# One row of a Fourier stage as three products side by side in column quarters, added up by a 96-row table in the next stage

## Chip, core, metric

The kernel runs on one core of one Trainium2 chip. The metric is the device time of one execution in microseconds (us), median of several. TensorE is called PE below, as in the profile; DVE is VectorE, ACT ScalarE, POOL GpSimd.

## The reference, cut to what matters

Block-sparse attention for 4 batches, 8 heads, 768 positions, head size 64; its output, 768 x 512 for each batch, then goes through a Fourier mix and a small network. Only the Fourier mix is touched:

```python
X = np.fft.fft(x, axis=1)            # along the sequence, 768
X = np.fft.fft(X, axis=2)            # across the model dimension, 512
mixed = np.real(X).astype(np.float32)
u = x + mixed
```

## The kernel before

For each batch, `along` multiplies folded inputs with cosine and sine tables of the sequence, and `across` multiplies the result with tables of the model dimension. Folding halves the columns twice; one column is left over, number QD = DM/4 = 128. Its row is called `side`, takes four products that accumulate, and enters `across` as a one-row product with the table `alt`. The parts concerned (cuts are marked):

```python
alt = const.tile([1, QD + 1], FP32, name="alt")
# ... setting up the tables, on VectorE:
for to, frm in ((dst, raw), (alt, row)):
    nc.vector.tensor_copy(out=to[:, 0:1], in_=frm[:, KD - 1:KD])
    nc.vector.tensor_copy(out=to[:, 1:QD + 1], in_=frm[:, 0:KD - 2:2])
# ...
parts = (slice(DM - QD, DM), slice(0, QD), slice(QD, QD + 1))
def along(g):                                   # g = 0, 1 cosine; 2, 3 sine
    # ...
    def cosine(ps, rows, cols):
        mm = nc.tensor.matmul
        for t in (0, 2):
            mm(ps[rows, 0:KS], sa[:, t, cols], cs_sb[:, t, :], start=(t == 0), stop=False)
        mm(ps[rows, 0:odd], e1[:, cols], cs_sb[:, 1, 0:odd], start=False, stop=False)
        mm(ps[rows, odd:KS], sa[:, 1, cols], cs_sb[:, 1, odd:KS], start=False, stop=True)
    # ...
    if g == 2:
        side = ps_m.tile([P, 512], FP32, tag="m", name="side")
        at = bank("m")
        cosine(side, slice(0, 1), parts[2])     # one column of weights
        st["zs"] = room(0, [P, 2, KS], "zs")
    # ... sine products into ps, copy of ps into zs
    if g == 2:
        keep_cosine(zs[0:1, 0, :], side[0:1, :])
        give(at, busy("PE", 2.0) + 1.5)

def across_p(ps, rows, ks):
    zc, zl = st["zc"], st["zs"][0:1, 0, :]
    mm = nc.tensor.matmul
    mm(ps[rows, 0:QD + 1], zc[:, 0, ks], cd_sb[:, 0:QD + 1], start=True, stop=False)
    mm(ps[rows, 0:QD + 1], zl[:, ks], alt, start=False, stop=True)
    mm(ps[rows, QD + 1:KD], zc[:, 1, ks], cd_sb[:, QD + 1:KD], start=True, stop=True)

def across(m):                                  # three planes of 128 positions
    # ...
    across_p(ps, slice(0, P), ks)
    if m == 1:
        end = ps_t.tile([P, 512], FP32, tag="t", name="end")
        across_p(end, slice(0, 1), slice(KS - 1, KS))   # the last row, by itself
```

## Time and profile before

| | before |
|---|---|
| median of the 3 runs at hand when predicting | 1147.89 us (1145.8 to 1148.28) |
| span of the profiled run | 1143.0 us |
| PE busy | 1091.1 us, 95% |
| VectorE, ScalarE, GpSimd busy | 56%, 34%, 22% |
| PE in the chain that ended last | 87% |

The page gives busy shares and the chain; the time view gives single stretches. The lines on which this rests are in the prediction, which also explains their columns.

### The profile page before, as it was taken

How to read it: one execution, taken by the hardware profiler on the slowest of the kernel's cores; microseconds unless marked ns; L12 is line 12 of the kernel's file. 1: busy time of each engine (PE TensorE's matmuls, PEld its weight loads, DVE VectorE, ACT ScalarE, POOL GpSimd, SP SyncE). 2: the span in 40 equal slices, each digit the busy share in tenths (PEclk: the TensorE clock that was granted, in tenths of full speed). 3: DMA queues.
4: the chain of work that ended last, by engine and by line, in shares of the span. 5: the costliest groups of instructions: out<-in, count | busy, mean ns of one | idle time of the engine just before them, and what ended most of it. 6: DMA issues, size and time to landing. Idle time of an engine off the chain costs nothing.

```text
span 1143.0 us, 11972 instructions
## 1 busy us (share of the span) xinstructions
PE 1091.1 (95%) x4284; PEld 518.3 (45%) x4284; DVE 643.2 (56%) x1190; ACT 391.6 (34%) x809; POOL 250.2 (22%) x182
## 2 busy tenths in 40 slices
PE   6999988979899999999999999999999999999997
PEld 2333333433445555454454555444444555544553
DVE  3888879488764544554459455544456355533431
ACT  3887755545212012344443112244330202201110
POOL 1000067457300000243536100243440001000000
PEclk9999999989899999999999999999999999999999
DMA  6657322011000000211111000111000001000002
GB/s 194 185 162 228 96 55 56 15 41 44 1 0 1 1 0 6 61 31 42 33 24 28 0 1 1 48 50 29 1 1 0 1 1 28 28 1 0 1 0 58
DMA packets 65184, 44.27 MB, mean 39 GB/s; under 512 B 52814, under 2 KB 57948, under 8 KB 65116
## 3 DMA queue, kind: packets, MB, share of 16 engines
q1 hardware_dynamic: 63228, 42.62, 13.1%
q10 hardware_dynamic: 1856, 0.79, 0.3%
q8 instruction: 36, 0.59, 0.2%
q14 instruction: 32, 0.26, 0.1%
q0 software_dynamic: 32, 0.01, 0.0%
HBM read 37.11 MB, written 6.29 MB: 38 GB/s over the span
## 4 chain that ended last, share of the span: by engine, by line
PE 87%; DVE 7%; ACT 3%; issue 2%; POOL 1%; DVEq 0%; ACTq 0%; POOLq 0%
PE y L932 29%; PE z L879 14%; PE s L468 11%; PE o L510 9%; PE yp L879 7%; PE xp L879 4%; DVE e L489 3%; PE tp L438 2%; PE zp L691 1%; PE sp L557 1%; PE xt L528 1%; PE s L473 1%; PE zp L669 1%; DVE x L744 1%; PE utp L806 1%
## 5 line engine op out<-in xcount | busy, mean ns | idle before, releaser
L498 POOL TENSOR_TENSOR acc<-acc,e 128x768 f32<-128x768 f32 x96 | 179.4, 1868 | 111.6 <-DVE e L489 107.0
L468 PE MATMUL s<-qT,kT 64*128 64x384 f32 x768 | 165.1, 535 | 13.9 <-DVE e L489 10.6
L935 DVE TENSOR_TENSOR x<-y,x 128x512 f32<-128x512 f32 x96 | 66.3, 691 | 196.6 <-PE y L932 196.4
L489 DVE TENSOR_TENSOR e<-s,mask 128x768 f32<-128x768 f32 x144 | 131.2, 951 | 73.9 <-ACT s L487 73.9
L932 PE MATMUL y<-w_sb,hB 128*128 128x512 f32 x384 | 170.2, 594 | 1.1 <-DVE x L935 1.0
L932 PE MATMUL y<-w_sb,hA 128*128 128x512 f32 x384 | 170.6, 593 | 0.6 <-ACT zs L693 0.6
L510 PE MATMUL o<-e,vr 128*64 128x384 f32 x768 | 146.1, 502 | 0.0
L487 ACT ACTIVATE s<-s 128x768 f32<-128x768 f32 x144 | 109.4, 794 | 68.4 <-PE s L468 67.3
L932 PEld LDWEIGHTS y<-w_sb,hB 128*128 128x128 f32 x384 | 71.5, 190 | 86.8 <-issue 81.9
L932 PEld LDWEIGHTS y<-w_sb,hA 128*128 128x128 f32 x384 | 71.2, 190 | 82.5 <-issue 79.5
L884 DVE TENSOR_TENSOR hA<-z,hA 128x384 f32<-128x384 f32 x64 | 35.7, 558 | 121.9 <-PE z L879 121.9
L496 POOL TENSOR_TENSOR acc<-e 128x768 f32<-128x768 f32 x24 | 46.3, 1928 | 248.8 <-DVE e L489 188.6
L468 PEld LDWEIGHTS s<-qT,kT 64*128 64x128 f32 x768 | 63.9, 190 | 74.9 <-DVE e L489 28.1
L879 PE MATMUL z<-unT,t 128*128 128x384 f32 x256 | 93.0, 486 | 0.0
L757 POOL TENSOR_SCALAR st<-st 128x1 f32<-128x1 f32 x24 | 6.6, 274 | 355.2 <-DVE st L756 354.8
L510 PEld LDWEIGHTS o<-e,vr 128*64 128x64 f32 x768 | 47.0, 137 | 76.8 <-issue 75.1
L888 ACT ACTIVATE hA<-hA 128x384 f32<-128x384 f32 x64 | 33.4, 522 | 119.4 <-DVE hA L884 118.8
L879 PEld LDWEIGHTS z<-unT,t 128*128 128x128 f32 x256 | 48.6, 190 | 33.9
L888 ACT ACTIVATE hB<-hB 128x384 f32<-128x384 f32 x64 | 33.5, 523 | 85.2 <-DVE hB L884 85.2
L899 ACT COPY hA<-xp 128x384 f32<-128x384 f32 x32 | 15.3, 478 | 134.4 <-PE xp L879 134.4
L879 PE MATMUL xp<-unT,w_sb 128*128 128x384 f32 x128 | 48.5, 502 | 1.5 <-ACT zs L693 1.1
L879 PE MATMUL yp<-unT,w_sb 128*128 128x384 f32 x128 | 47.1, 491 | 0.2 <-DVE un L726 0.2
(173 smaller groups left out, 1243.1 us busy)
## 6 DMA issues: line engine op xcount, KB each, us to landing
wraw<-in_moe_w_ch_dram SPq DMA_DIRECT2D x32, 512.0 KB
qr<-in_q_dram SPq DMA_DIRECT2D x90, 64.0 KB
vr<-in_v_dram SPq DMA_DIRECT2D x30, 192.0 KB
kr<-in_k_dram SPq DMA_DIRECT2D x28, 192.0 KB
out_dram<-x SPq DMA_DIRECT2D x16, 128.0 KB
out_dram<-x SPq DMA_DIRECT2D x8, 256.0 KB
out_dram<-x SPq DMA_DIRECT2D x8, 126.0 KB
out_dram<-x SPq DMA_DIRECT2D x4, 252.0 KB
```

Of the source, the lines that this page charges most:

```text
L438: nc.tensor.transpose(tp[:, c * P:(c + 1) * P], part, ident)
L468: nc.tensor.matmul(s[:, i, 0:HS], kT[D * i:D * i + D, c * P:(c + 1) * P], qT[D * i:D * i + D, half * HS:(half + 1) * HS], start=True, stop ...
L487: nc.scalar.activation(out=s[:, :, 0:HS], in_=s[:, :, 0:HS], func=ACT.Exp, scale=scale)
L489: nc.vector.tensor_tensor(out=e, in0=s[:, :, 0:HS], in1=m.broadcast_to([P, 2, HS]), op=ALU.mult)
L496: nc.gpsimd.tensor_add(out=acc_of[n, half], in0=e_of[u - 1], in1=e)
L498: nc.gpsimd.tensor_add(out=acc_of[n, half], in0=acc_of[n, half], in1=e)
L510: nc.tensor.matmul(o[D * i:D * i + D, :], vt[:, i, c, :], e[:, i, :], start=(c == 0), stop=(c == C - 1))
L879: nc.tensor.matmul(to, a[:, k, :], c[:, k, :], start=(k == 0), stop=(k == ND // 2 - 1))
L884: tt(out=to, in0=ps, in1=a, op=ALU.add)
L888: nc.scalar.activation(out=h, in_=h, func=ACT.Relu)
L932: nc.tensor.matmul(y, hs[half][:, l, m * P:(m + 1) * P], w2_sb[:, 4 * r + l, :], start=(l == 0), stop=(l == 3))
L935: nc.vector.tensor_tensor(out=x[:, m, :], in0=y, in1=x[:, m, :], op=ALU.add)
```

## The change

The four products of `side` no longer accumulate in one output. The first two and the pair of half-length ones go to three quarters of the array's columns (output partitions 0, 32 and 64), where they can run at once; 32 weight columns each are loaded, of which one matters. The three partial rows are added by the next stage's product: `alt` gets 96 rows, with the table in rows 0, 32 and 64 and zeros elsewhere. The intent is to shorten the 2 us of `side`.

```diff
-    alt = const.tile([1, QD + 1], FP32, name="alt")
+    alt = const.tile([96, QD + 1], FP32, name="alt")
...
-                for to, frm in ((dst, raw), (alt, row)):
+                nc.vector.memset(alt, 0.0)
+                for to, frm in ((dst, raw), *((alt[g:g + 1, :], row) for g in (0, 32, 64))):
...
-                cosine(side, slice(0, 1), parts[2])
-                st["zs"] = room(0, [P, 2, KS], "zs")
+                for i, (lhs, t, cols) in enumerate(((sa[:, 0, :], 0, slice(0, KS)),
+                                                    (sa[:, 2, :], 2, slice(0, KS)),
+                                                    (e1, 1, slice(0, odd)),
+                                                    (sa[:, 1, :], 1, slice(odd, KS)))):
+                    g32 = 32 * min(i, 2)
+                    nc.tensor.matmul(side[g32:g32 + 32, cols], lhs[:, QD:QD + 32],
+                                     cs_sb[:, t, cols], start=True, stop=True,
+                                     tile_position=(0, g32))
+                st["zs"] = room(0, [P, 3, KS], "zs")
...
-                keep_cosine(zs[0:1, 0, :], side[0:1, :])
-                give(at, busy("PE", 2.0) + 1.5)
+                keep_cosine(zs[0:96, 2, :], side[0:96, :])
+                give(at, busy("PE", 0.8) + 1.5)
...
-            zc, zl = st["zc"], st["zs"][0:1, 0, :]
+            zc, zl = st["zc"], st["zs"][0:96, 2, :]
```

More of the change, by code (lines that the diff above doesn't have):

```diff
@@ L653, in fourier @@
                  lambda: fold_1(1), lambda: fold_2(0), lambda: fold_2(2), lambda: fold_2(1)]
-        parts = (slice(DM - QD, DM), slice(0, QD), slice(QD, QD + 1))
+        parts = slice(DM - QD, DM), slice(0, QD)
         def along(g):
```

## The prediction

> **What bounds the kernel now.** I read the page first: the busy shares and the chain that ended last.
>
> ```profile
> PE 1091.1 (95%) x4284; PEld 518.3 (45%) x4284; DVE 643.2 (56%) x1190; ACT 391.6 (34%) x809; POOL 250.2 (22%) x182
> ...
> PE 87%; DVE 7%; ACT 3%; issue 2%; POOL 1%; DVEq 0%; ACTq 0%; POOLq 0%
> ```
>
> TensorE (PE) is busy in 95% of 1143.0 us and carries 87% of the chain. A microsecond taken from it should mostly come off the end, except where it waits for someone else. I took the busy time by stretches to see where that is.
>
> ```profile
> 180.00:370.00 190.00, 170.11 (x729) 83.26 (x728) 132.08 (x199) 73.92 (x159) 74.70 (x49) 0.96 0.09 21
> 370.00:560.00 190.00, 189.39 (x692) 92.07 (x690) 93.71 (x181) 54.27 (x110) 43.58 (x34) 1.00 0.10 25
> 560.00:860.00 300.00, 296.61 (x1156) 143.70 (x1154) 162.98 (x275) 100.19 (x207) 97.66 (x61) 1.00 0.07 18
> 860.00:940.00 80.00, 79.02 (x240) 40.72 (x241) 40.32 (x91) 11.02 (x27) 1.56 (x4) 1.00 0.00 1
> ```
>
> After the length of a stretch comes busy PE. From 370 us on, PE is 99% busy; only 180 to 370 us has 20 us of PE idleness. The changed code runs once per batch: batch 0 at 203 to 261 us, inside that loose stretch; batches 1, 2 and 3 at 338 to 387, 638 to 687 and 888 to 937 us, in full ones (at 338 to 387 us PE waits once, 0.57 us).
>
> Next, PE in order of time around one `side` (the single row DM/4), batch 3. Columns: start, length to the end of the last matmul, line, rows*columns of the weights, shape, count. An fp32 matmul shows as two passes. I use differences of starts, because ends overlap.
>
> ```profile
> 902.21 1.45 PE L879 MATMUL z<-unT,t 128*128 128x384 f32 x4
> 903.59 1.45 PE L669 MATMUL side<-cs_sb,sa 128*1 128x385 f32 x4
> 904.89 0.49 PE L670 MATMUL side<-cs_sb,e 128*1 128x192 f32 x2
> 905.21 0.49 PE L671 MATMUL side<-cs_sb,sa 128*1 128x193 f32 x2
> 905.63 2.20 PE L691 MATMUL zp<-sn_sb,sd 128*128 128x384 f32 x6
> ```
>
> One useful weight column holds PE from 903.59 to 905.63: 2.04 us. Then PE around the next stage, one plane with the extra row `end`:
>
> ```profile
> 934.05 0.39 PE L701 MATMUL pq<-cd_sb,zc 128*128 128x129 f32 x2
> 934.36 0.48 PE L702 MATMUL pq<-alt,zs 1*128 1x129 f32 x2
> 934.78 0.49 PE L703 MATMUL pq<-cd_sb,zc 128*128 128x128 f32 x2
> 935.20 0.38 PE L701 MATMUL end<-cd_sb,zc 128*1 128x129 f32 x2
> 935.51 0.38 PE L702 MATMUL end<-alt,zs 1*1 1x129 f32 x2
> 935.81 0.38 PE L703 MATMUL end<-cd_sb,zc 128*1 128x128 f32 x2
> 936.12 0.49 PE L716 MATMUL pq<-sd_sb,zs 128*128 128x127 f32 x2
> 936.45 0.39 PE L718 MATMUL pq<-sd_sb,zs 128*128 128x128 f32 x2
> 936.67 1.13 PE L879 MATMUL xp<-unT,w_sb 128*128 128x384 f32 x3
> ```
>
> Two passes of 128 columns from L718 to the next line take 0.22 us (936.45 to 936.67). The same work around the one-row `alt` product takes 0.31, 0.42 and 0.42 us: PE loses time wherever the weights' shape changes, about 0.1 us before and 0.1 us after.
>
> **What the Trainium skill says.** "TensorEngine Tiling (Array Packing)", Key Properties, says that different tiles load and multiply in parallel and that changing the tiling mode, not just the tile, drains TensorE. The trace agrees: 0.22 against 0.42 us above. The built program gives `alt` a 32x128 tile before and 128x128 after, its neighbours 128x128 in both; for `end`, 32x32 becomes 128x32, again as its neighbours have. "TensorE: Matmul & The Clock Gate", Part 3, Measured speedup, gives 2.38x for three column tiles of 32. This trace has four such tiles:
>
> ```profile
> 48.79 0.85 PE L557 MATMUL sp<-e,pick 128*32 128x384 f32 x8
> 49.58 0.33 PE L314 MATMUL m<-at_q,at_k 24*128 24x384 bf16 x1
> ```
>
> Eight passes of 384 columns in 0.79 us; one after another they would take 8 x 0.3225 = 2.58 us (0.3225 is the spacing in the `side` row: (904.89 - 903.59) / 4), so 3.3x with four different moving operands. The same page, LDWEIGHTS, has load time go by the columns of the weights, not by the rows contracted. The trace agrees: 181 ns for the 1x128 loads of `alt`, 190 for 128x128 ones. So 96 rows in place of one should cost some 9 ns a load.
>
> **The change part by part.**
> 1. `side`. Removed, per batch: 2.04 us. Added: three products in column quarters 0, 1 and 2, two of 385 columns, and 192 then 193 columns in the third. Each quarter streams two passes of 385 columns' worth, 2 x 0.3225 = 0.645 us. Adding the exposed weight load and drain that `sp` shows (0.79 - 0.645 = 0.14) gives 0.79 us if all three run beside each other. If the third quarter's passes had to keep order with the others, I estimate its four would end about 0.16 us later, 0.95 us. I take 0.81: saved 1.23 us, four times, **4.9 us**.
> 2. `alt` in the planes. L701, L702, L703 now have one mode. A plane that follows 128x128 work and precedes L716 takes 0.31 + 0.42 + 0.32 = 1.05 us before (the last without the drain towards `end`); with six passes at 0.108 it takes 0.65. Saved 0.40 us; the drain towards `end` and entries from 128x64 work stay and cancel. Three planes, four batches: 12 x 0.40 = **4.8 us**. The diff does not mention this; it comes from the tile size alone.
> 3. `alt` in `end`: 0.31 + 0.31 + 0.31 becomes 0.22 + 0.22 + 0.31, 0.18 us x 4 = **0.7 us**.
> 4. ScalarE copies `side` out with 96 rows for one: 480 ns where it was 470, 263 where 252 (`zc`'s 128-row copies against `zs`'s one-row copies). About 20 ns a batch, beside PE.
> 5. VectorE at about 132.8 us: a memset of 96x129 and four more small copies. Each existing pair starts 0.2 us after the one before; with 0.2 assumed for the memset, 0.6 us once, in a stage where VectorE runs ahead of what PE needs. I charge 0.3.
>
> The order of instructions on all engines in the part that runs is otherwise unchanged: the scheduler's smaller figure for `side` (0.8 for 2.0) reorders nothing there. Sum on PE: 4.9 + 4.8 + 0.7 = 10.4 us.
>
> **What of it reaches the end.** Batches 1 to 3 stand in full PE work: all 3 x 2.6 = 7.8 us. In batch 0 the chain in order of time goes through PE from 200 to 223 us, through `side` and the first plane, then by ScalarE to VectorE's mask product; both start earlier, so 1.6 us should pass. The second plane at 237.5 us leads into GpSimd's sums and statistics, the third at 258 us is on PE's chain: I count half of the second and all of the third, 0.2 + 0.6. Sum: 7.8 + 2.4 - 0.3 = 9.9 us; I take off another 0.4 for waits that reappear: **9.5 us**, 1147.89 - 9.5 = 1138.4 us, 0.8%.
>
> **The rivals.**
> - *The packing doesn't pack.* Had the two products in the third quarter, or three weight loads of 32 columns, to run one after another, `side` would stay near 2.0 us and only the 5.5 us of mode changes would come: about 1143 us. Against it: `sp` packs already.
> - *Only packing counts, mode changes are no loss.* If the 0.1 us before and after `alt` came from the accumulation or the read of the one-row tile and not from its shape, the planes would keep 1.05 us: 4.9 us saved, about 1143.5 us. Against it: `end`, surrounded by other shapes, shows the same 0.1 us at each of its edges.
> - *A wait takes its place.* After `side`, PE waits for the copy of `zs` (0.57 us in batches 1 and 3), and before 300 us scores wait for VectorE's mask product:
>
> ```profile
> PE s L468 <- DVE e L489: 10.6, 9, 1.9
> ```
>
> If VectorE, 98% busy from 224 to 236 us, sets the pace of batch 0, most of its 2.6 us is lost: 1140.5 us. For it: the chain is on VectorE for part of this stage. The 0.57 us wait is a fixed distance behind the sine product and moves with it.
> - *The clock.* PE idleness near 245 us coincides with a granted clock of 0.81 from 248 to 262 us. Shifting it may move the time 1 to 2 us either way.
>
> **Range and chances.** The gain runs from about 5 (one of the first two rivals) to about 11 us (all passes, no loss), and the runs of the kernel before spread by 2.5 us. I say 1138.4 us, 8 in 10 between 1134.0 and 1143.5. Two per cent is 23 us, more than twice all the PE time at stake, so faster by over 2% gets 0.01; slower by over 2% would need a new stall of 23 us with the order unchanged, 0.01.
>
> **What would show it.** In the changed profile: from the start of `side` to the start of the sine product 0.75 to 0.95 us where it was 2.04; in the planes 0.22 us (0.31 after 128x64 work) from the `zc` product to `alt`, 0.22 from `alt` to the next, and no 0.42; in `end` the first two steps 0.22; PE busy some 9 to 11 us lower; the wait after the sine product still about 0.57 us; 20 us of PE idleness in the 180 to 370 us stretch grown by no more than about 1 us. The prediction is wrong if `side` keeps 2 us, if planes keep 1.05 us, or if idle time before scores grows by what PE saved.

## The result, and the profile after

The changed kernel took 1133.82 us (median of 4 runs, 1131.42 to 1136.86) against 1146.85 us (4 runs, 1143.91 to 1148.28): ratio 0.9891, 95% interval 0.9859 to 0.9923. A ratio here is the mean time of one kernel's fast runs over the mean of the other's in the same rounds, so not quite the ratio of the medians.

First the page of the changed kernel: PE's share stays at 95%, with 11.7 us less busy time.

```profile
PE 1079.4 (95%) x4284; PEld 516.3 (46%) x4284; DVE 643.9 (57%) x1195; ACT 391.4 (35%) x809; POOL 250.1 (22%) x182
```

Then PE in order of time around `side` of batch 3:

```profile
895.23 0.52 PE L695 MATMUL side<-cs_sb,sa 128*32 128x385 f32 x2
895.24 0.51 PE L695 MATMUL side<-cs_sb,e 128*32 128x192 f32 x2
895.57 0.51 PE L695 MATMUL side<-cs_sb,sa 128*32 128x385 f32 x4
896.01 2.20 PE L701 MATMUL zp<-sn_sb,sd 128*128 128x384 f32 x6
898.78 0.70 PE L942 MATMUL y<-w_sb,hA 128*128 128x512 f32 x1 [0.57 <-ACT zs L703]
```

Two first passes of 385 columns and the third quarter's first start within some 20 ns (895.23, 895.24); the long quarters' second passes follow at 895.57, and the sine product starts at 896.01: 0.78 us after `side` began, where it was 2.04. The wait after the sine product is still 0.57 us. And the planes of batch 3, with the first rows of `end`:

```profile
923.65 0.39 PE L711 MATMUL pq<-cd_sb,zc 128*128 128x129 f32 x2
923.88 0.39 PE L712 MATMUL pq<-alt,zs 96*128 96x129 f32 x2
924.10 0.39 PE L713 MATMUL pq<-cd_sb,zc 128*128 128x128 f32 x2
924.41 0.38 PE L711 MATMUL end<-cd_sb,zc 128*1 128x129 f32 x2
924.63 0.39 PE L712 MATMUL end<-alt,zs 96*1 96x129 f32 x2
```

The steps are 0.23 and 0.22 us where they were 0.31 and 0.42. The `alt` weights are now 96*128 for 1*128 and cost no more. The 0.31 us before `end`, whose single column is still another shape, is left.

To see where the 10.8 us between the two traces come from, I cut each at fixed instructions (starts read from the views by time). A slot is one step of the attention loop. The same was done for a second trace of each, taken later:

| stretch | before | after | difference | second pair |
|---|---|---|---|---|
| start to the third slot's first scores | 25.00 | 22.10 | -2.90 | -2.06 |
| to `side` of batch 0 | 185.95 | 186.73 | +0.78 | +1.67 |
| to `side` of batch 1 | 140.66 | 139.47 | -1.19 | -2.86 |
| to `side` of batch 2 | 299.75 | 297.28 | -2.47 | -2.47 |
| to `side` of batch 3 | 252.24 | 249.65 | -2.59 | -2.58 |
| to the end of batch 3's planes | 33.08 | 30.49 | -2.59 | -2.59 |
| to the end | 206.29 | 206.43 | +0.14 | +0.18 |
| sum | 1142.96 | 1132.15 | -10.82 | -10.71 |

Two things stand out. Batches 1 to 3 give nearly the same amount each. And the first 25 us, in which nothing was changed, give more than any batch. That, and the loss just after it, had to be explained.

### The profile page after: what moved, and what is told of

Its sections match the earlier page's. It is cut to its first block, busy times and chain, and to the rows that moved or that the text cites. A ratio compares the mean times of both kernels' runs of the same rounds, so it can differ in the third digit from the quotient of the medians.

```text
span 1132.1 us, 11978 instructions
## 1 busy us (share of the span) xinstructions
PE 1079.4 (95%) x4284; PEld 516.3 (46%) x4284; DVE 643.9 (57%) x1195; ACT 391.4 (35%) x809; POOL 250.1 (22%) x182
## 4 chain that ended last, share of the span: by engine, by line
PE 85%; DVE 8%; ACT 2%; issue 2%; DMA 1%; SPq 1%; POOL 1%; ACTq 0%; DVEq 0%; POOLq 0%
PE y L942 29%; PE z L889 15%; PE s L470 10%; PE o L512 8%; PE yp L889 7%; PE xp L889 4%; DVE e L491 3%; PE tp L440 2%; PE zp L701 1%; PE sp L559 1%; DMA wraw<-in_moe_w_ch_dram 1%; PE xt L530 1%; PE zp L672 1%; PE s L475 1%; PE sp L573 1%
```

## The experiments

**My theory.** The change takes about 2.6 us of PE time a batch in two parts that have nothing to do with each other: packing (1.25 us) and the end of shape changes around `alt` (1.33 us). The rest of the first rounds' 13 us is chance in the start-up. **Rivals.** Packing alone is the gain; shape changes alone are it; the start-up belongs to the change. All runs have 5 rounds beside the kernel before.

| run | median us (range), 6 runs | ratio to before (95%) |
|---|---|---|
| after_again | 1134.76 (1133.7 to 1137.28) | 0.9926 (0.9904 to 0.9948) |
| before_again | 1141.61 (1141.17 to 1144.52) | 0.9984 (0.9962 to 1.0005) |
| pack_only, wrong result | 1140.79 (1137.06 to 1146.37) | 0.9973 (0.9945 to 1.0001) |
| mode_only | 1138.14 (1135.8 to 1141.58) | 0.9957 (0.9932 to 0.9981) |
| flat | 1137.93 (1135.22 to 1138.33) | 0.9937 (0.9914 to 0.9960) |
| end_wide | 1136.24 (1132.76 to 1138.17) | 0.9927 (0.9903 to 0.9952) |
| warm | 1131.25 (1130.05 to 1135.76) | 0.9899 (0.9873 to 0.9924) |
| best | 1131.83 (1129.34 to 1136.97) | 0.9901 (0.9874 to 0.9928) |
| pool_alt | 1134.61 (1131.75 to 1137.16) | 0.9902 (0.9871 to 0.9932) |
| best_all | 1129.74 (1128.8 to 1131.72) | 0.9863 (0.9834 to 0.9893) |
| warm_before | 1139.94 (1139.05 to 1143.64) | 0.9964 (0.9933 to 0.9996) |

The first four rows share a chip and its runs of before (11, median 1144.02), the next four another (1144.52), the last three a third (1144.55).

### after_again and before_again: the two kernels once more

No edit. 

> The changed kernel once more, unaltered. Theory: the change takes 10.5 us of TensorE time (4 x 1.25 in the side row, 12 x 0.40 in the planes, 4 x 0.18 in the end row), of which 9.5 to 10.5 us reach the end, so a ratio of 0.990 to 0.992; the 12.5 us of the first rounds holds 2 to 3 us of run-to-run start-up difference, already there in the two traces before the first changed instruction (side of batch 0 starts at 208.8 us against 210.95). Rival: the change is worth 12.5 us or more by itself, ratio 0.989 again.

> The kernel before against itself, for the size of the noise and for a second trace of it. Theory: ratio 1.000 within 0.003; the start of batch 0's side row in this trace differs from 210.95 us by up to 2 or 3 us although nothing was changed, and the distances within batches 1 to 3 are the same to 0.05 us. Rival: batch 0's side row starts at 210.9 again, and then the changed kernel's earlier start has to be explained by the change.

The changed kernel came out at 0.9926, 8.5 us, a little short of the expected 0.990 to 0.992, which the interval of 5.9 to 11 us still holds; before against itself at 0.9984. Over all rounds and chips, the 10 runs of the changed kernel have a mean of 1134.70 us and the 43 of before 1144.21: 9.5 us. The runs of before go from 1141.2 to 1149.0. That the start of before's trace would differ was a miss: batch 0's `side` began at 210.84 us, after 210.95 in the first trace. On that reading my start-up theory could have fallen. But the changed kernel's two traces differ among themselves (208.83 and 210.45 us), and the next runs' traces have 212.07 and 207.67, above and below both. `warm` and `warm_before` below settled it.

### pack_only: packing without the shape

```diff
-            zc, zl = st["zc"], st["zs"][0:96, 2, :]
+            zc, zl = st["zc"], st["zs"][0:1, 2, :]
-            mm(ps[rows, 0:QD + 1], zl[:, ks], alt, start=False, stop=True)
+            mm(ps[rows, 0:QD + 1], zl[:, ks], alt[0:1, :], start=False, stop=True)
```

> The changed kernel with the next stage's product on one row of the packed result only (so a wrong result on purpose): the three products side by side stay, the 32x128 tile of the row product returns. Theory of two separate parts: side row 0.78 us, row product with 0.42 us steps again; 4.5 to 5 us faster than before, ratio 0.9957. Rival that the packing is the whole gain: ratio 0.989 to 0.991 as the whole change. Rival that mode changes are the whole gain: ratio 1.000.

`side` took 0.78 us, and the planes looked as before the change (PE in order of time, batch 3):

```profile
931.27 0.39 PE L711 MATMUL pq<-cd_sb,zc 128*128 128x129 f32 x2
931.59 0.48 PE L712 MATMUL pq<-alt,zs 1*128 1x129 f32 x2
932.00 0.49 PE L713 MATMUL pq<-cd_sb,zc 128*128 128x128 f32 x2
```

The result is wrong, as meant (relative error 0.045). The ratio, 0.9973, is about 3 us; 4.5 to 5 were expected, which the interval holds. The interval excludes the rival that packing is the whole gain, but it reaches 1.0001, so the time alone does not exclude the rival of no gain. The trace does: from `side`'s start to the end of its planes, batches 1 to 3, it saves 1.25 us each (table after the next run).

### mode_only: the shape without packing

```diff
-    alt = const.tile([1, QD + 1], FP32, name="alt")
+    alt = const.tile([96, QD + 1], FP32, name="alt")
-                for to, frm in ((dst, raw), (alt, row)):
+                nc.vector.memset(alt, 0.0)
+                for to, frm in ((dst, raw), (alt[0:1, :], row)):
-                st["zs"] = room(0, [P, 2, KS], "zs")
+                st["zs"] = room(0, [P, 3, KS], "zs")
+                nc.scalar.copy(out=st["zs"][0:96, 2, :], in_=st["zc"][0:96, 0, :])
-                keep_cosine(zs[0:1, 0, :], side[0:1, :])
+                keep_cosine(zs[0:1, 2, :], side[0:1, :])
-            zc, zl = st["zc"], st["zs"][0:1, 0, :]
+            zc, zl = st["zc"], st["zs"][0:96, 2, :]
```

> The kernel before with the side row's four products one after another as they were, but its product in the next stage taken over 96 rows, 95 of them against zeros of the table (right result; one more ScalarE copy of 96x385 per batch fills those rows). Theory: side row 2.04 us as before; row product 0.22 us steps in the planes; 5 to 5.5 us faster, ratio 0.9953. Rival that the packing is the whole gain: 1.000, with 0.42 us steps left, which would then come from the accumulation and not from the tile's shape.

`side` took 2.04 us again, and the planes of batch 3 were:

```profile
925.83 0.39 PE L703 MATMUL pq<-cd_sb,zc 128*128 128x129 f32 x2
926.06 0.39 PE L704 MATMUL pq<-alt,zs 96*128 96x129 f32 x2
926.28 0.39 PE L705 MATMUL pq<-cd_sb,zc 128*128 128x128 f32 x2
```

The same accumulation into the same output, with the same number of instructions, takes 0.22 us steps once its weights have 96 rows, 95 of them worth nothing. So the 0.42 us came from the shape. The ratio, 0.9957, is some 5 us, as expected.

From `side`'s start to the end of its batch's planes, in us:

| | batch 1 | batch 2 | batch 3 |
|---|---|---|---|
| before | 35.24 | 35.24 | 33.08 |
| pack_only | 33.99 | 33.99 | 31.82 |
| mode_only | 33.97 | 33.91 | 31.74 |
| after | 32.65 | 32.66 | 30.49 |

In batch 3 the parts are 1.25 and 1.33 us and the whole is 2.59: they add up.

### flat: no packing, one shape throughout

As mode_only without its extra ScalarE copy; `side` computes 96 columns to have its neighbours' shape (the lines that differ from mode_only):

```diff
-        parts = (slice(DM - QD, DM), slice(0, QD), slice(QD, QD + 1))
+        parts = (slice(DM - QD, DM), slice(0, QD), slice(QD, QD + 96))
-                cosine(side, slice(0, 1), parts[2])
+                cosine(side, slice(0, 96), parts[2])
-                keep_cosine(zs[0:1, 0, :], side[0:1, :])
+                keep_cosine(zs[0:96, 2, :], side[0:96, :])
```

> The kernel before with the side row's four products one after another, but with 96 weight columns (95 of them not needed) so that they have the full-array shape of their neighbours, and the row product over 96 rows against 95 zeros of the table; right result. Theory that changes of shape cost TensorE about 0.1 us before and up to 0.1 us after, whatever the work: side row 1.93 us instead of 2.04, the step before it 0.32 instead of 0.41 and the sine product's first step 0.32 instead of 0.43; so 1.2 us more than mode_only, in all 6.5 us faster than before, ratio 0.9943; from side's start to the end of the batch's planes 33.7 us in batches 1 and 2 (35.24 before, 33.97 mode_only). Rival that the row's one column was the cheap thing and 96 columns cost more: 35 us or more.

```profile
897.20 1.45 PE L880 MATMUL z<-unT,t 128*128 128x384 f32 x4
898.49 1.46 PE L670 MATMUL side<-cs_sb,sa 128*96 128x385 f32 x4
...
900.44 0.81 PE L692 MATMUL zp<-sn_sb,sd 128*128 128x384 f32 x2
```

Four passes before `side` now take 1.29 us (897.20 to 898.49) where they took 1.38, and `side` itself 1.95 for 2.04. Batches 1 to 3 take 33.78, 33.71 and 31.55 us. Computing 95 columns that nobody wants made the row cheaper, because it saved two changes of shape. The ratio, 0.9937, is close to the expected 0.9943.

### end_wide: the shape change that the change left

```diff
+            cut = (lambda ap: _run(ap, KS - 1, 128, 0)) if ks is None else (lambda ap: ap[:, ks])
-            mm(ps[rows, 0:QD + 1], zc[:, 0, ks], cd_sb[:, 0:QD + 1], start=True, stop=False)
+            mm(ps[rows, 0:QD + 1], cut(zc[:, 0, :]), cd_sb[:, 0:QD + 1], start=True, stop=False)
... (the other two products likewise)
-                across_p(end, slice(0, 1), slice(KS - 1, KS))
+                across_p(end, slice(0, 128), None)
```

> The changed kernel with the end row's weights read as 128 copies of its one column (step 0), so that it too has the full-array shape; right result. Theory: end's three steps 0.22 each instead of 0.22, 0.22, 0.31, the steps before and after it 0.22 instead of 0.32; 0.28 us a batch, side's start to end of planes 32.37 us instead of 32.65; 1.1 us in all, below what the times can show against the changed kernel, ratio to before about 0.990. Rival: reading one column 128 times makes the weight load slower, steps of 0.3 us or more.

```profile
926.60 0.39 PE L712 MATMUL end<-cd_sb,zc 128*128 128x129 f32 x2
926.83 0.39 PE L713 MATMUL end<-alt,zs 96*128 96x129 f32 x2
927.05 0.39 PE L714 MATMUL end<-cd_sb,zc 128*128 128x128 f32 x2
927.27 0.39 PE L727 MATMUL pq<-sd_sb,zs 128*128 128x127 f32 x2
```

All steps are 0.22 us, and the three batches take 32.38, 32.38 and 30.21: another 0.28 us each, as expected to 0.01. In the times, 0.9927 where about 0.990 was expected, it is lost in the spread.

### warm and best: is the start a matter of PE's speed?

In the traces the same four score passes take 1.65 us or 0.92 us in the first 25 us. PE in order of time of the kernel before, and the busy time of the stretch, whose third column from the right is the granted clock:

```profile
17.97 1.65 PE L468 MATMUL s<-qT,kT 64*128 64x384 f32 x4
```

```profile
15.00:20.00 5.00, 5.00 (x19) 1.73 (x17) 0.00 (x0) 2.93 (x5) 0.00 (x0) 1.00 1.03 326
```

And the corresponding passes of the changed kernel:

```profile
16.62 0.92 PE L470 MATMUL s<-qT,kT 64*128 64x384 f32 x4
```

Half speed ended at 14.9 us in the first trace of the changed kernel, at 16.8 in the second and in mode_only, at 21.3 in both of before, at 22.6 in pack_only. The 1.00 in the clock column does not contradict this: in each of these traces the first clock record is the rise to full speed at just that moment, and the column shows 1.00 where there is no record. Why the rise comes early in one execution and late in another is not shown. The experiment gives PE something to do in its idle time before:

```diff
+    spun = w2_sb[:, NF - 1, :]
+    nc.vector.memset(spun, 1.0)
...
+    def spin(n):
+        idle = ps_m.tile([P, 512], FP32, tag="m", name="idle")
+        for _ in range(n):
+            nc.tensor.matmul(idle[:, 0:448], spun[:, 0:P], spun[:, 0:448], start=True, stop=True)
+    spin(3)
     turn(0, 1, 0)
     turn(0, 0, 0)
+    spin(2)
```

> The changed kernel with five products of constants in TensorE's idle time of the first 11 us, result not read. Theory that the traces' different starts come from how long TensorE runs at half speed after its first work: the score passes from 11 us on take 0.92 us for four from the start, where they took 1.65 us until 15 to 22 us in the traces so far; the third slot's scores start at 20 to 21 us instead of 22 to 25.6 us, the runs spread less, and the time falls by another 2 to 4 us: ratio to before 0.987 to 0.989. Rival that the half speed belongs to the operands or the weight loads of these first slots: 1.65 us as before, no gain.

With `warm`, four passes at 11.10 us took 0.92 us, the third slot began at 20.39 us, and the median was 1131.25 us, 0.9899. The speed is therefore not the operands' doing. Its ratio just misses the expected 0.987 to 0.989, and lies between the two that the changed kernel had in other rounds (0.9891 and 0.9926); in the same rounds its mean is 3.7 us below that of end_wide (1132.2 and 1135.8), which has no constants. The runs did not spread less: 5.7 us, against the changed kernel's 5.4 and 3.6. `best` is warm with end_wide:

> The changed kernel with both, the end row in the full-array shape and the products of constants at the start. If the two add up: 1.1 us from the first and 2 to 4 us from the second on top of the change's 10 us, ratio to before about 0.987. If the start-up products don't help: about 0.990.

It measured 0.9901, no better than warm, and its range was 7.6 us: a miss for the sum. Its trace, of one execution, shows a part of the reason: the constants ended earlier, PE then idled for 2.37 us, and half speed was back until 14.6 us. The third slot began at 22.00 us, 1.6 us later than in `warm`.

```profile
11.11 1.63 PE L472 MATMUL s<-qT,kT 64*128 64x384 f32 x4 [2.37 <-DVE qT L450]
```

In this trace the clock records begin at 4.35 us, during the constants. So here the clock column (0.66) does show the half speed; the record itself has 0.50 from 11.17 to 14.59 us:

```profile
10.00:15.00 5.00, 3.89 (x13) 1.25 (x14) 1.28 (x9) 0.81 (x1) 0.00 (x0) 0.66 0.68 173
```

So what the score passes lose at the start is the granted clock.

### pool_alt: where the loss after the start comes from

In the changed kernel PE waits near 142 us for VectorE's first mask product of the second stage:

```profile
141.89 1.78 PE L470 MATMUL s<-qT,kT 64*128 64x384 f32 x8 [0.66 <-DVE e L491]
```

In before's trace the same passes start at 144.19 us with no wait noted.

```diff
-                nc.vector.memset(alt, 0.0)
+                nc.gpsimd.memset(alt, 0.0)
...
-                    nc.vector.tensor_copy(out=to[:, 0:1], in_=frm[:, KD - 1:KD])
-                    nc.vector.tensor_copy(out=to[:, 1:QD + 1], in_=frm[:, 0:KD - 2:2])
+                    eng = nc.vector if to is dst else nc.gpsimd
+                    eng.tensor_copy(out=to[:, 0:1], in_=frm[:, KD - 1:KD])
+                    eng.tensor_copy(out=to[:, 1:QD + 1], in_=frm[:, 0:KD - 2:2])
```

> The changed kernel with the table for the row (its memset and six small copies) made on GpSimd, which is idle then, instead of VectorE. Theory: VectorE works without a break from about 20 us to the first mask product of the second stage, so the 0.6 us of set-up that the change added there push that product back, and TensorE waits 0.66 us for it near 141 us where it had not waited before; on GpSimd they don't, the wait is gone (0.1 us or less; VectorE has even 0.2 us less to do than before the change), and from the scores of the third slot to the 25th unit pair of the second stage it is 119.0 to 119.2 us as before the change, not 119.75 to 119.79. Total 0.6 us, not to be seen in the times: ratio to before 0.990 to 0.992. Rival: the wait comes from something else and stays.

```profile
144.47 1.78 PE L471 MATMUL s<-qT,kT 64*128 64x384 f32 x8
```

The wait is gone. From the third slot's scores to those of slot 25 (the interval that the expectation means; slots counted from 0) it is 119.13 us, as in before's two traces (119.19 and 119.13), against 119.79 and 119.75 in the two of the changed kernel, 119.74 in pack_only and 119.78 in end_wide, all with the full set-up. mode_only and flat, which add the memset alone, have 119.13 and 119.18. So the set-up's four more copies cost 0.6 us on the path. The time ratio, 0.9902, can't show it. One detail of the expectation is wrong: VectorE does pause, ten times for 13.1 us in all between 25 and 145 us of before's trace; but the last pause of note (2.04 us) ends at 126.6 us, and the set-up comes after it. The set-up also leaves 0.2 and 1.1 us of the loss before batch 0 unexplained (0.78 and 1.67 in the table).

### best_all and warm_before: the start by itself, and everything together

best_all is the changed kernel with end_wide, pool_alt and `spin(3)`, `spin(4)` in place of `spin(3)`, `spin(2)`. warm_before is the kernel before with the same seven products.

> The changed kernel with the end row in full-array shape, the table made on GpSimd, and seven products of constants in the first 11 us instead of five (four instead of two in the second gap, where TensorE fell back to half speed in the run called best). Theory: all score passes from 11 us on at 0.92 us for four; third slot's scores at 20.4 us; ratio to before 0.985 to 0.988, and a smaller spread than the 7.6 us of best. Rival: more products delay the first scores, or half speed comes back: 0.990 as best.

> The kernel before with the same seven products of constants at the start and nothing of the change. Theory: the start-up is a matter apart from the change: 3 to 4.5 us faster than before, ratio 0.996 to 0.9975, third slot's scores at 20.4 us in place of 25.0. Rival: no gain, 1.000.

```profile
11.17 0.92 PE L473 MATMUL s<-qT,kT 64*128 64x384 f32 x4
```

In both, the third slot starts at 20.4 us (20.46 and 20.39). best_all has the lowest median of all, 1129.74 us, 0.9863, and its six runs lie within 2.9 us. warm_before comes to 0.9964, some 4 us faster, with nothing of the change in it; its runs still fall into two groups (1139.1 to 1140.0 and 1143.5 to 1143.6), so the start is not the whole spread. The start-up is a matter apart, worth almost half as much as the change.

## Why the prediction was right or wrong

- **`side`** was put at 0.81 us and measured 0.784 in all four batches. What sets it are the two long quarters, 0.35 and then 0.44 us to the next product; the third quarter's four passes hide beside them. The 0.95 us case, with passes kept in order, did not occur. (Two figures of the prediction do not follow from its lines: a pass of `side` is 1.30 / 4 = 0.325 us, not 0.3225, and one of 128 columns 0.22 / 2 = 0.11, not 0.108. That moves the 4.8 us for the planes by 0.1 us and no other sum by as much.)
- **The planes** were put at 0.40 us each and gave 0.386: the six passes take 0.668 us, not 0.65. **`end`** was put at 0.18 and gave 0.174. With 1.254 for `side` the sum is 4 x 1.254 + 12 x 0.386 + 4 x 0.174 = 10.3 us of PE work, against 10.4 predicted. mode_only shows that half of it came from the tile's shape, as the prediction said and the diff does not. PE's busy time fell by 11.7 us, more than the 9 to 11 named as a sign; it counts passes at half speed at their full length, so it is not a pure sum of work.
- **Batches 1 to 3** were to give 7.8 us and gave 2.47 + 2.59 + 2.59 = 7.6 to the next fixed points in the first pair of traces.
- **Batch 0** was to give 2.4 us. It gave 1.2 in one pair of traces and 2.9 in the other. In the first changed trace the second plane ran at half speed (steps of 0.43 to 0.59 us at 234 us), in the second it didn't. The prediction's fourth rival, the clock, is what shows; how much of the 2.4 us would pass at an equal clock stays open.
- **The set-up** was the mis-sized term: 0.6 us of work was counted rightly, but half of it was taken to lie in slack ("VectorE runs ahead of what PE needs", 0.3 charged). It all reached PE, as a wait of 0.66 us at 142 us. VectorE had no slack left there: in before's trace it rounds weights from 126.6 us on without a pause of note until that mask product at 143.2 us, and the set-up (132.6 us) falls into this stretch.
- **The wait after the sine product** stayed at 0.57 us, and no new wait took the place of the removed work apart from the set-up's. In the stretch from 180 to 370 us PE is idle 19.8 us (170.16 of 190 busy), as before (170.11).
- **The total**: 9.5 us was predicted, and 9.5 us is the difference of the means over all rounds. So exact an agreement is partly luck: the first rounds gave 13 us and the second 8.5, and without the first 25 us, where nothing was changed, the two pairs of traces differ by 7.9 and 8.7 us. The absolute 1138.4 us was 4.6 us too high, and the measured 1133.82 us lies 0.2 us below the low end, although the ratio 0.9891 applied to the 1147.89 us that the prediction started from gives 1135.4, within the range. Two causes: the three runs at hand for before were among its longer ones (its 43 runs have a mean of 1144.2 us), and the prediction allowed 1 to 2 us for the clock, only in the middle of the run. The first 25 us alone moved by 3.8 us between traces without the constants (22.1 to 25.9 us). More of the spread goes with the clock: where the record lists it, before's runs above 1148 us all have a mean of 0.987, those below 1142 us 0.990 to 0.993. That the clock is the cause is not shown.

## What to carry to other kernels

Read a small product's cost between starts, with its neighbours: a one-row or one-column product can cost more in changes of shape on both sides than in passes, and padding it to the neighbours' shape, or reading one column 128 times, can be cheaper than the small form. Before sizing a gain of 1%, look at how far the runs of the old kernel spread and where in the trace they part, and compare distances between fixed instructions instead of ends. Set-up work is free only if the engine it lands on has a pause before the first thing that others wait for.

## What the Trainium skill lacked or had wrong

- "TensorEngine Tiling (Array Packing)", Key Properties, says that changing the mode drains TensorE, without a size. Here it is about 0.09 to 0.1 us on the step before the change (1.38 for 1.29 us ahead of `side`), and up to 0.1 us after it: 0.32 for 0.22 us for the 128-column product after `end`, next to nothing for a one-column product.
- "TensorE: Matmul & The Clock Gate", Part 3, The mechanism, says that matmuls start and end in program order. Here an fp32 product shows as two passes, and the third product's two started at 895.24 and 895.43 us, before the second passes of the first two at 895.57. In what order the passes were issued the trace does not tell; product by product, the order is not kept.
- The same page, Part 1, has full speed come about 4 us into sustained work, within half a microsecond from run to run. Here half speed lasted from the first scores at 11.1 us until between 14.9 and 23.2 us (the latest in flat), 3.8 to 12.1 us later, with PE at work all the while. In `best` it returned after an idle time of 2.37 us; in `warm`, after 1.54 us, it did not.
- On no page: the profile's clock column reads 1.00 until the trace's first clock record, which is the rise itself (21.34 us in before's trace), though the passes ahead of it take 1.65 us instead of 0.92.
